# Decay rows of a pair loaded for both heads in one transfer: two transfers a pair instead of four

## The chip, the cores and the metric

One core of a Trainium2 chip runs the whole program. The time is the device time of one execution in microseconds; each version is run several times and the median counts. The engines are named as in the profile: PE is TensorE (matrix multiplications), with PEld for its weight loads; DVE is VectorE, ACT is ScalarE, POOL is GpSimd. SP is SyncE, which in this kernel does nothing but issue DMA transfers (its queue is SPq in the trace).

## The reference, cut to what matters

Three stages follow each other: causal attention with a decay, a feed-forward layer with a leaky ReLU, and a second layer with a softmax-gated activation and a layer norm. There are 4 batches of 8 heads, a sequence of 576 and a head dimension of 64; the 2304 tokens then go through matrices of 512 x 2048, 2048 x 512, 512 x 1024 and 1024 x 512. The change lies in the scores of the attention:

```python
scores = scale * np.matmul(q, k.transpose(0, 1, 3, 2))
log_f = np.log(np.clip(f, 0.0001, 1.0))
cum = np.cumsum(log_f, axis=-1)
decay = cum[:, :, :, None] - cum[:, :, None, :]
scores = np.where(causal, -1000000000.0, scores + decay)
scores = scores - np.max(scores, axis=-1, keepdims=True)
attn = np.exp(scores)
```

The decay of a score is a sum of a term of its query and a term of its key. So it can be had from the same matrix product that gives the scores, by a few more rows under the 64 rows of Q and K: these are the decay rows.

## The kernel before, in words

**Pairs and blocks.** The 32 heads are worked on in 16 pairs (two heads of one batch). A head's 576 queries are five blocks of 128 (the last has 64). Blocks 0 and 1 need only the first 256 keys. A pair is worked on twice: once for blocks 0 and 1 (pass kind "A", called full, since its scores are plain f32 matmuls), once for blocks 2, 3 and 4 (kind "B", called split: Q and K are split in two parts of lower precision first). `PASSES` (L41) lists eight passes of four pairs each, one for each batch and kind, with the priority of its first pair and the step from pair to pair: ("A", 0, 127.52, 0.5), ("A", 1, 186, 3), ("B", 0, 200, 5), ("A", 2, 222, 8), and so on. Pair 7 is the last pair of ("A", 1).

**Decay rows.** `decay()` (L504) computes the cumulative logarithms of all heads once and writes them to a tensor in DRAM, `dr_d` (L383), with four rows for each head: high and low parts of the decay, and ones, so laid out that the same four rows serve keys and queries in different columns. `row(h, p)` (L498) gives the index in `dr_d` of head h of pair p. The four writes are kept in `st["cols"]`, on which every load of decay rows depends.

**Loads of a full pair.** `prep_full` (L566) takes the four pairs of batch 0 from a tile of their own, `qa`, and returns. For the other 12 pairs it takes a `raw` tile (there are three, `NRAW`, L28), loads 64 rows of Q and K for both heads by one transfer from `kqa` (L575; 256 KB), and then rows 64 to 67 by four transfers from `dr_d` (L576 to L579): for each head one for the 256 keys (columns 0 to 255) and one for the 256 queries (columns 256 to 511), 4 KB each. The scores' matmuls (`qk_mm`, L639) then read 68 rows of one head's half of the tile. `raw` tiles are also what the split pairs (`prep_split`, L582) load their Q and K into (`raw<-kq`, 480 KB), and what stages weights later on. They are handed out in the order in which the code asks for them.

**What sets the order.** The code above issues nothing by itself. Each step is an operation in a `Plan` (L112) with an engine or a choice of engines, an expected duration, a priority and its dependences. `Plan.run` (L163) plays them through with its own model of time, and emits each instruction when the model gives it an engine: of those that are ready, the one with the lowest priority number, if its tiles can be had. That order of emission is each engine's order on the chip, where each engine and each DMA queue goes strictly in order. A transfer (`move`, L462; `load`, L466) takes 475 ns of SP in the model (L463), and at least 460 ns lie between two transfers (L289). A transfer is passed over while more than `BACKLOG` (L54) of expected DMA time is queued (L258), unless its priority is below -1000. A load's priority is that of its pair less `LD` = 51.31 (L48); that of a weight less `LDW` = 52.07 (L50); spills of results have the pair's less 400 and the transposes (`turn`, L469, used in `softmax`, L686) that less 500. All transfers go through SP (`QUEUES`, L99).

**Weights.** `load_wi` and `load_wo` (L821, L825) load weights of 512 KB through three `wst` tiles and turn them to two parts on ACT, DVE and POOL; chunk c has the priority 137.84 + 5.27 c (`wi`) or 148.79 + 5.27 c (`wo`), c up to 8 in the first half (L1037 to L1040). `ffn_a` (L891) computes the feed-forward layer's first half from them, between the attention's work.

Of the kernel before, what the change touches and what calls it, by code (L numbers as in the profile page):

```python
# [47 lines left out]
LD = 51.31  # L48
# [14 lines left out]
KB = CQ + 256  # L63
# [294 lines left out]
def body(tc, kqa, kq, vt, f, wa, w2i, w2o, gln, out):  # L358
# [24 lines left out]
    dr_d = dram.tile([2 * NP, 4, KQ], F32, name="dr_d")  # L383
# [78 lines left out]
    def move(dst, src, nbytes, prio, engs=QUEUES, **kw):  # L462
        d = {SP: 475.0, ACT: 490.0, POOL: 1040.0}  # L463
        return flex(engs, [d[e] for e in engs], lambda e: queue[e].dma_start(dst(), src()), prio, dma=nbytes / 360.0, **kw)

    def load(buf, dst, src, nbytes, prio, mode="w", **kw):  # L466
        return move(dst, src, nbytes, prio, **{mode: [buf]}, **kw)
# [30 lines left out]
    def row(h, p):  # L498

        return KD * h + p if p < KD else 2 * KD + (NP - KD) * h + p - KD  # L500
# [57 lines left out]
    st, QK, VT, U, QA = {}, {}, {}, {}, {}  # L558
# [7 lines left out]
    def prep_full(p, prio):  # L566


        if p < KD:
            bq = QA[0]  # L570
            QK[p] = [[(bq, p), (bq, "n"), (bq, "c")]] * 2, lambda hd: qa[0:66, hd, p], {0: 256, 1: 384}
            return
        bq = P.buf("raw")
        a = lambda r0, r1: bq.t[r0:r1, 0:1024].rearrange("r (h c) -> r h c", h=2)
        load((bq, 0), lambda: a(0, 64), lambda: kqa[p].rearrange("(h d) c -> d h c", h=2), 64 * 1024 * 4, prio - LD)  # L575
        for hd in range(2):  # L576
            for c0, k0 in ((0, 0), (256, KB)):
                load((bq, (hd, c0)), lambda hd=hd, c0=c0: a(64, 68)[:, hd, c0:c0 + 256], lambda hd=hd, k0=k0: dr_d[row(hd, p), :, k0:k0 + 256], 4096, prio - LD,
                     deps=st["cols"])  # L579
        QK[p] = [[bq]] * 2, lambda hd: a(0, 68)[:, hd], {0: 256, 1: 384}  # L580

    def prep_split(p, prio):  # L582
# [562 lines left out]
```

## Time and profile before

| | |
|---|---|
| Median of 3 runs | 848.83 us (846.91 to 849.77) |
| The profiled execution's own time | 848.65 us |
| Its span, first to last instruction | 846.9 us |
| PE busy | 767.9 us, 91% |
| DVE, ACT, POOL busy | 519.4, 490.1, 348.8 us |
| Mean granted clock of PE | 0.993 of full speed |
| DMA, mean | 128 GB/s, 52.3% of 16 engines' span |
| Decay loads `raw<-dr_d` | 48 of 4 KB |

The span is that of one profiled execution. Busy time is the time in which an engine has an instruction under way; an idle time is put down to the instruction or transfer whose end released the engine. Numbers in a row of the trace are microseconds unless they are marked ns. In the names, `raw<-dr_d` is a transfer into a `raw` tile from `dr_d`; `pt<-hl` is a transpose of softmax results.

### The profile page before, as it was taken

The numbers are of one execution on the slowest core, as the hardware profiler recorded it, in microseconds if no ns is written. First come the engines' busy times: TensorE is split into PE (matmuls) and PEld (weight loads), VectorE is DVE, ScalarE is ACT, GpSimd is POOL, SyncE is SP. The second block draws the span as 40 slices with busy tenths as digits, with TensorE's granted clock in tenths as the row PEclk, the third lists the DMA queues.
The fourth block names the chain that finished last, engine by engine and source line by source line (L and its number), as shares of the span: only waits on it lengthen the run. The fifth ranks groups of instructions, "written<-read, shape, count | busy, mean of one in ns | idle before, by whom it ended". The sixth has DMA issues, their size and how long they took to land.

```text
span 846.9 us, 16019 instructions
## 1 busy us (share of the span) xinstructions
PE 767.9 (91%) x5648; PEld 695.5 (82%) x5648; DVE 519.4 (61%) x1350; ACT 490.1 (58%) x1242; POOL 348.8 (41%) x448
## 2 busy tenths in 40 slices
PE   1753798979999999999899998999999999999996
PEld 1432698968998999999899987898889988998885
DVE  5788767888888878884654667334633434253551
ACT  4886768889889889884555543232333243333321
POOL 6648545166618564822610443422332233222321
PEclk9999999989999999999999999999999999999999
DMA  8997457687789677694655643321332131312223
GB/s 230 220 223 245 96 130 151 150 221 154 136 162 216 155 163 151 174 160 148 195 172 177 189 104 104 71 79 16 98 71 68 26 87 38 87 26 63 26 56 82
DMA packets 184402, 108.37 MB, mean 128 GB/s; under 512 B 150033, under 2 KB 167137, under 8 KB 184321
## 3 DMA queue, kind: packets, MB, share of 16 engines
q1 hardware_dynamic: 184320, 107.35, 52.3%
q8 instruction: 44, 0.72, 0.4%
q14 instruction: 38, 0.30, 0.1%
HBM read 57.39 MB, written 14.78 MB: 85 GB/s over the span
## 4 chain that ended last, share of the span: by engine, by line
PE 64%; DMA 10%; DVE 9%; ACT 8%; issue 4%; POOL 3%; SPq 0%; ACTq 0%; DVEq 0%; POOLq 0%
PE ps_f L473 40%; PE ph L473 10%; PE py L473 6%; PE ps_s L473 5%; PE ps_v L473 3%; ACT ps_s L657 2%; DMA raw<-w2o 2%; DMA tr<-hl 2%; DMA raw<-kq 2%; DMA wst<-wa 1%; DMA pt<-hl 1%; ACT hl L427 1%; DVE hl L438 1%; DMA qa<-sd 1%; DVE ps_s L707 1%
## 5 line engine op out<-in xcount | busy, mean ns | idle before, releaser
L473 PE MATMUL ps_f<-x,wi 128*128 128x256 f32 x972 | 131.7, 289 | 1.2 <-POOL x L442 1.1
L473 PE MATMUL ps_f<-g,wo 128*128 128x256 f32 x972 | 126.4, 284 | 2.5 <-DVE g L855 2.5
L473 PEld LDWEIGHTS ps_f<-x,wi 128*128 128x128 f32 x972 | 124.7, 193 | 3.1 <-POOL x L442 1.9
L473 PEld LDWEIGHTS ps_f<-g,wo 128*128 128x128 f32 x972 | 120.8, 188 | 4.0 <-DVE g L855 2.9
L473 PE MATMUL ph<-wi,g 128*128 128x512 f32 x408 | 98.5, 397 | 1.4 <-DVE raw L968 1.4
L473 PE MATMUL ps_f<-x,wib 128*128 128x256 f32 x756 | 97.3, 279 | 1.8 <-DVE g L855 1.7
L438 DVE SCALAR_TENSOR_TENSOR hl<-ps_s,st,hl 128x512 f16<-128x512 f32 (+4 forms) x160 | 82.8, 540 | 19.4 <-ACT hl L427 16.5
L473 PEld LDWEIGHTS ps_f<-x,wib 128*128 128x128 f32 x756 | 91.6, 188 | 2.9 <-DVE g L855 2.8
L473 PEld LDWEIGHTS ph<-wi,g 128*128 128x128 f32 x408 | 75.9, 188 | 19.3 <-DVE raw L968 1.6
L855 DVE TENSOR_TENSOR g<-ps_f,g 128x256 fp32r<-128x256 f32 x144 | 60.3, 420 | 48.1 <-ACT ps_f L854 47.2
L853 ACT ACTIVATE g<-ps_f 128x256 fp32r<-128x256 f32 x144 | 54.8, 380 | 59.3 <-PE ps_f L473 58.1
L657 ACT ACTIVATE ps_s<-ps_s,st 128x512 f32<-128x512 f32 (+4 forms) x160 | 78.6, 491 | 10.1 <-DVE st L707 6.1
L473 PE MATMUL ps_f<-wo,x 128*128 128x512 f32 x348 | 84.0, 396 | 0.0
L427 ACT ACTIVATE hl<-ps_s,st 128x512 f16<-128x512 f32 (+4 forms) x151 | 76.1, 532 | 11.6 <-DMA pt<-hl 4.7
L473 PE MATMUL ps_v<-pt,VT 128*128 128x128 f16 (+1 forms) x928 | 62.3, 220 | 20.0 <-DVE xr L742 9.0
L473 PE MATMUL py<-g,wob 128*128 128x256 f32 x567 | 75.6, 278 | 2.0 <-ACT g L427 2.0
L473 PEld LDWEIGHTS ps_f<-wo,x 128*128 128x128 f32 x348 | 64.8, 188 | 15.1
L473 PE MATMUL ps_s<-kq 128*128 128x512 f32 (+5 forms) x256 | 66.7, 380 | 11.6 <-DVE hl L438 5.5
L442 POOL TENSOR_TENSOR kq<-raw,kq 64x576 fp32r<-64x576 f32 (+1 forms) x53 | 67.9, 1283 | 21.5 <-ACT kq L427 15.2
L473 PEld LDWEIGHTS <-VT 128*128 128x128 f16 x928 | 50.0, 102 | 30.4 <-issue 15.4
L473 PEld LDWEIGHTS py<-g,wob 128*128 128x128 f32 x567 | 71.2, 188 | 4.3 <-ACT g L427 2.3
L707 DVE CUSTOM_DVE_ANT_0 ps_s<-ps_s,mask 128x256 f32<-128x256 f32 (+3 forms) x128 | 62.2, 496 | 5.9 <-PE ps_s L473 4.5
(159 smaller groups left out, 1221.7 us busy)
## 6 DMA issues: line engine op xcount, KB each, us to landing
wst<-wa SPq DMA_DIRECT2D x18, 512.0 KB
sd<-xs_d SPq DMA_DIRECT2D x32, 256.0 KB
raw<-kq SPq DMA_DIRECT2D x16, 480.0 KB
raw<-wa SPq DMA_DIRECT2D x14, 512.0 KB
raw<-yp_d SPq DMA_DIRECT2D x18, 256.0 KB
vr<-vt SPq DMA_DIRECT2D x13, 320.0 KB
raw<-w2i SPq DMA_DIRECT2D x8, 512.0 KB
raw<-w2o SPq DMA_DIRECT2D x8, 512.0 KB
```

The lines of the kernel that those rows point to most:

```text
L427: nc.scalar.activation(o, i, CP, scale=1.0 if scale is None else scale)
L438: nc.vector.scalar_tensor_tensor(o, a, scale, b, op0=ALU.mult, op1=ALU.subtract)
L442: (nc.vector if eng == DVE else nc.gpsimd).tensor_tensor(o, a, b, op=ALU.subtract)
L473: nc.tensor.matmul(o, lhsT=l, rhs=r, start=start, stop=stop)
L657: P.op(ACT, act(W, 1, True) + 93, lambda view=view, j=j, k=k: nc.scalar.activation(view(), view(), AF.Exp, bias=sts.t[:, j:j + 1], scale=- ...
L707: P.op(DVE, dve(W) + 130, lambda i=i, j=j, view=view: nc.vector.tensor_tensor_reduce(view(), view(), mask[:, 512 - 128 * i:640], -0.125, 3 ...
L853: P.op(ACT, act(n, 0, True), lambda: nc.scalar.activation(g.t[:, 0, 0:n], h(), AF.Prelu, scale=WSC, alpha=0.01), eprio, w=[(g, 0)], r=[ps])
L855: P.op(DVE, dve(n) + 60, lambda: nc.vector.tensor_tensor(g.t[:, 1, 0:n], h(), g.t[:, 0, 0:n].bitcast(F32), op=ALU.subtract), eprio, w=[(g, ...
```

## The change

The loop over the two heads goes. Keys and queries are each loaded for both heads by one transfer, from a slice of `dr_d` that takes the rows of head 0 and head 1 of the pair by a step, turned so that the four rows are outermost. The tile, its layout, the bytes, the priority and the dependences are the same; the two transfers are of 8 KB.

```diff
-        for hd in range(2):
-            for c0, k0 in ((0, 0), (256, KB)):
-                load((bq, (hd, c0)), lambda hd=hd, c0=c0: a(64, 68)[:, hd, c0:c0 + 256], lambda hd=hd, k0=k0: dr_d[row(hd, p), :, k0:k0 + 256], 4096, prio - LD,
-                     deps=st["cols"])
+        for c0, k0 in ((0, 0), (256, KB)):
+            load((bq, c0 + 1), lambda c0=c0: a(64, 68)[:, :, c0:c0 + 256], lambda k0=k0: dr_d[row(0, p):row(1, p) + 1:row(1, p) - row(0, p), :, k0:k0 + 256].rearrange("h r c -> r h c"),
+                 8192, prio - LD, deps=st["cols"])
```

## Rows read from the trace of the kernel before

**Rows 1.** Busy time by stage: stage, length, engines with instruction counts, granted clock, DMA.
```profile
58.00:65.00 7.00, 0.83 (x3) 0.57 (x4) 4.62 (x13) 5.76 (x16) 2.81 (x4) 1.00 0.97 308
65.00:92.00 27.00, 9.50 (x31) 5.77 (x30) 21.76 (x52) 17.72 (x38) 20.72 (x19) 1.00 0.63 205
...
172.00:204.00 32.00, 25.98 (x194) 22.63 (x191) 25.97 (x83) 27.50 (x77) 21.07 (x24) 0.84 0.84 197
...
275.00:400.00 125.00, 124.41 (x1183) 119.16 (x1183) 97.05 (x285) 102.92 (x276) 62.52 (x76) 1.00 0.70 156
...
500.00:820.00 320.00, 316.54 (x1968) 281.04 (x1967) 145.85 (x274) 108.37 (x234) 97.10 (x142) 1.00 0.27 62
```

In a row of this view the busy times are those of PE, PEld, DVE, ACT and POOL in this order; after them come the granted clock, the DMA engines' busy share and GB/s.

**Rows 2.** Waits of PE over the whole span: total, times, longest.
```profile
PE ps_s L473 <- DMA raw<-dr_d: 6.2, 1, 6.2
```

**Rows 3.** Timeline of PE, 57 to 93 us: start, length, instructions, idle before.
```profile
57.79 0.74 PE L473 MATMUL ps_s<-raw 68*128 68x128 f32 x2
64.69 2.48 PE L473 MATMUL ps_s<-raw 68*128 68x128 f32 x6 [6.17 <-DMA raw<-dr_d]
69.73 0.79 PE L473 MATMUL ps_s<-kq 128*128 128x512 f32 x1 [2.56 <-ACT kq L427]
...
92.41 2.91 PE L473 MATMUL ps_f<-x,wi 128*128 128x256 f32 x12
```

**Rows 4.** Timeline of SP's queue, 47 to 63 us: start and length of issues.
```profile
47.80 0.98 SPq L464 DMA_DIRECT2D wst<-wa  x2
48.87 0.67 SPq L464 DMA_DIRECT2D raw<-kqa  x1
49.59 0.48 SPq L464 DMA_DIRECT2D raw<-dr_d  x1
...
50.56 0.32 SPq L464 DMA_DIRECT2D raw<-dr_d  x1
...
57.74 0.33 SPq L464 DMA_DIRECT2D raw<-dr_d  x1
...
61.66 0.33 SPq L464 DMA_DIRECT2D raw<-dr_d  x1
62.04 0.34 SPq L464 DMA_DIRECT2D raw<-kq  x1
```

**Rows 5.** Waits of SP's queue from 18 to 66 us, the largest.
```profile
SPq L470 <- DVE hl L438: 5.2, 6, 1.6
```

**Rows 6.** The chain that ended last: start, length, what.
```profile
48.40 6.38 DMA wst<-wa
...
62.04 4.58 DMA raw<-kq
```

**Rows 7.** Issue durations on SP by transfer: ns min/median/max, first and last start.
```profile
L464 SPq DMA_DIRECT2D raw<-dr_d x48: 239/290/483, 20.8 to 250.6; - x48
...
L464 SPq DMA_DIRECT2D raw<-kqa x12: 607/640/672, 11.2 to 247.2; - x12
...
L464 SPq DMA_DIRECT2D sd<-xs_d x48: 359/419/1712, 63.2 to 725.8; - x48
...
L464 SPq DMA_DIRECT2D qa<-sd x2: 688/752/817, 7.3 to 10.2; - x2
```

**Rows 8.** Timelines of SP's queue and of PE, 97 to 260 us.
```profile
101.30 0.65 SPq L464 DMA_DIRECT2D raw<-dr_d  x2
...
161.15 0.39 PE L473 MATMUL ps_s<-raw 68*128 68x128 f32 x2
...
172.97 0.99 SPq L464 DMA_DIRECT2D raw<-kq  x1
...
250.08 0.81 SPq L464 DMA_DIRECT2D raw<-dr_d  x2
...
258.59 0.49 PE L473 MATMUL ps_s<-raw 68*128 68x128 f32 x2 [0.18 <-DVE hl L438]
```

## The prediction, made before the change was run

> **What bounds the kernel now.** I began with the share of busy time stage by stage [rows 1]. From 275 to 400 us TensorE is busy 124.41 of 125.00 us, and from 500 to 820 us 316.54 of 320.00: there the end is set by TensorE's own matmuls, and nothing that a load of 4 KB does can shorten them. What can be won lies where TensorE idles: 6.17 us of the stretch 58 to 65 us (it is busy 0.83 of 7.00), 17.50 us of 65 to 92 us, and 6.02 us of 172 to 204 us, where the granted clock's mean is also down to 0.84, so that part of the stretch ran on the lower of the two levels, after TensorE had begun to idle.
>
> Next, what TensorE waited for [rows 2]. Of all its waits, one is put down to a decay-row load: 6.2 us, once. So of the 48 loads of `raw<-dr_d`, at most the last one or two of one pair have ever held the matmuls up. TensorE's timeline [rows 3] gives the place. At 57.79 us it computes a first block of pair 7, the last of the four pairs of pass ("A", 1); then it idles 6.17 us until 64.69 and goes on with that pair's other three blocks. SyncE's timeline [rows 4] says why: pair 7's Q and K load goes out at 48.87, its four decay loads at 49.59, 50.56, 57.74 and 61.66. The first two are head 0's, the last two head 1's, which come 8 to 12 us later. The last lands some 3.0 us after its issue (61.66 to 64.69).
>
> Why so late? SyncE is not full: between 18 and 66 us it waits itself, most of all for the low halves of the softmax (`hl`) that its transposes move [rows 5]. The plan is what holds the loads back. It lets a transfer go only when its own account of queued DMA time is under BACKLOG (9115 ns, L258), and then the lowest priority number first. Pair 7's loads have 186 + 3 x 3 - 51.31 = 143.69. The weights come before them (`wi` up to 137.84 + 5.27 x 8 - 52.07 = 127.93, `wo` up to 138.88), and so do transposes and spills; the first split load `raw<-kq` of pass ("B", 0) has 148.69 and comes after them. Each decay load of pair 7 thus uses one of few openings, and the issue of `raw<-kq` follows directly behind the fourth one, at 62.04 [rows 4]. That load is on the chain that ended last [rows 6].
>
> **The change part by part.**
>
> Removed and added: 12 pairs x 4 issues of 0.290 us go, 12 x 2 issues of two heads come [rows 7]. No row shows the new form (4 partitions, two heads, 256 elements). Its bounds: 0.290 us, if a second head costs nothing, and 0.752 us, the dearest row of a form with more dimensions (`qa<-sd`). The row nearest in pattern is `raw<-kqa`, 0.640 us, since it too takes heads out of the outer dimension of DRAM; nearest in the piece of a partition is `sd<-xs_d`, 0.419 us, two pieces of 256 elements. I take the middle of these two, 0.53 us. With 0.05 us between issues a pair saves 4 x 0.34 - 2 x 0.58 = 0.20 us of SyncE (bounds: 0.68 saved, 0.24 lost; over 12 pairs +8.2 to -2.9 us). SyncE has waits of its own around most of these, which cover either sign; if that cover were gone, the -2.9 us would be the loss. On the chain stands one such issue alone, at 61.66 with its gap: 62.04 - 61.66 = **0.4 us** gained.
>
> Pair 7's wait: if the two new loads go where the first two went, the second is out by about 51 us. Ahead of it are the weights issued at 47.80; the chain has a weight transfer from 48.40 to 54.78 [rows 6]. Landing behind that and with the 3.0 us seen, it is there by 55 to 58 us, before TensorE's turn at 58.5 (64.69 - 6.17). So the 6.17 us wait goes. What is late next: `ACT kq`, for which TensorE waits until 69.73 [rows 3]. The idle time on TensorE is therefore not what is gained. Gained is that the softmax of three blocks moves to a stretch where its engines had room: from 58 to 65 us VectorE idles 7.00 - 4.62 = 2.38 us, ScalarE 1.24 us, while from 65 to 92 us VectorE is busy 21.76 of 27.00 us and passes everything that the first feed-forward matmul (92.41 us) needs. At best 2.4 us, at worst nothing; I take the smaller room, ScalarE's, **1.2 us**.
>
> The split load `raw<-kq`: two openings of the plan come free, so it may go at 57.74 instead of 62.04, 4.3 us earlier. But DMA is busy 0.97 of that stretch at 308 GB/s [rows 1]; 480 KB brought forward push the weights behind by 480/308 = 1.6 us. So 0 to 2.7 us; I take the middle, **1.4 us**.
>
> The other eight pairs of the passes ("A", 2) and ("A", 3): nothing waits for them. Pair 8's last decay load goes out at 101.30 us and its first matmul is at 161.15; even the last pair's (250.08) are 8.5 us before a matmul on `raw` at 258.59 [rows 8]. Gain or loss 0 beyond SyncE's time above; the cover is that the loads are early.
>
> Moved: everything, a little. The plan books 475 ns of SyncE and 460 ns of its DMA queue for each transfer (L463, L289), so 24 transfers are 11.4 us fewer in SyncE's planned time, and from the first of them (20.8 us [rows 7]) on all queues may be put in another order. The trace has no row for that; its bounds are those of the largest stall in the mixed stage, 172 to 204 us: 6.0 us given back or a second 6.0 us. I take 0.
>
> Sum: 0.4 + 1.2 + 1.4 = 3.0 us of the profiled execution's 848.65 (span 846.9, and 1.75 around it), 845.65. That execution lies 0.2 us under the median of 848.83, so against the runs 845.8. Bounds without a new order: 848.8 and 848.8 - 5.5 = 843.3.
>
> **The rivals.**
>
> (a) The whole wait comes off: after 92 us TensorE is dense, so if the feed-forward began 6.2 us earlier, the end would too: 842.6. For it: VectorE and ScalarE have idle time before 92 us. Against: the wait for `ACT kq`, and the 17.50 us idle up to 92 that no decay load causes.
> The Trainium skill, page "DMA: Bandwidth & Descriptors", section "Rules for kernel authors", says that many small transfers are to be joined, since under 64 KB one pays mostly overhead; its fit (section on the GpSimd path's DMA) has some 2.0 us fixed for each, which for 24 would be, as an estimate, 48 us. The trace disagrees with that as a price of time: 47 of 48 decay loads have no wait of TensorE to their name.
>
> (b) No change: VectorE, at 81% from 65 to 92 us, takes as long for its work whatever pair 7 does, and the weights pushed behind `raw<-kq` take back the rest; or the new issues cost 0.6 to 0.75 us and nothing is saved, so that the change halves a count and not a time: 848.8, 847 to 850.
>
> (c) Slower: another order of the queues makes a second gap like that of 172 to 204 us. There `raw<-kq`, issued at 172.97 [rows 8], came when TensorE had run out of what was ready; its slot of `raw` comes free only after the last matmul of a pair that held it. If the new order puts that last matmul, or a transpose, one turn later in front of such a load at another place, TensorE idles 6.0 us once more: 854.8; with the clock's share of that stretch (0.16 x 32.00 = 5.1 us at most) 859.9. It decides from the point where idle time of TensorE between 92 and 275 us grows by more than the 3.0 us won before 92. For it: the plan doesn't know the real landings; it put head 1's matmul of pair 7 where TensorE then stood 6.17 us. Against: a new order can as well ease that gap, and before 92 us the change only takes work from a queue.
>
> **How the numbers follow.** The forecast, 845.8, has 0.30; (a) 0.10; (b) 0.28; (c) 0.32. A measurement of this kernel can tell about 0.3%, 2.5 us, from no change; the forecast and (a) lie beyond it: faster 0.40, same 0.28, slower 0.32. The likeliest case's own range is 843.3 to 847.5. The whole range starts 2 us under (a), for an order that also eases the gap at 172 us, 840.5, and ends at 857, half way through (c)'s two prices: beyond these lie less than 2 in 10.
>
> **What would show it.** Right: 24 `raw<-dr_d` of 8 KB; no wait of TensorE on `raw<-dr_d` about 58 us; `raw<-kq` out before 62 us; the first feed-forward matmul some 3 us before 92.41; TensorE's busy time unchanged at 768. Issues of 0.5 to 0.6 us would bear out my price. Wrong: a first feed-forward matmul at 92 or later, or one earlier whose lead is gone by 275 us, with longer idle and a clock under 1.00 in the mixed stage; or a wait on `raw<-dr_d` still there, because the plan puts both loads late.

## The result, and the profile after

The changed kernel is slower: 856.51 us (median of 4 runs, 855.29 to 857.56) against 847.87 us for the kernel before (845.01 to 849.77). The ratio is 1.0104, with a 95% interval of 1.0068 to 1.0140. The profiled execution took 855.29 us, its span 853.5. One execution among all those below, the first of the kernel with four early transfers, took 1289.13 us at a mean granted clock of 0.626 and is left out of that kernel's figures.

What the change says it does, it does. First the issue durations of the changed kernel on SP's queue (ns min/median/max), to be read beside [rows 7]:

```profile
L464 SPq DMA_DIRECT2D raw<-dr_d x24: 242/318/547, 19.7 to 248.0; - x24
```

24 transfers in place of 48, and one with two heads takes 0.318 us where one with a single head took 0.290. Next SP's queue about 50 us, which answers to [rows 4] (start, length):

```profile
47.26 0.66 SPq L464 DMA_DIRECT2D raw<-kqa  x1
47.96 0.82 SPq L464 DMA_DIRECT2D raw<-dr_d  x2
...
51.64 0.38 SPq L464 DMA_DIRECT2D raw<-kq  x1
...
60.65 0.42 SPq L464 DMA_DIRECT2D raw<-kq  x1
```

All decay rows of pair 7 are out by 48.8 us, and the first split load goes out at 51.64 instead of 62.04. And PE's timeline, beside [rows 3]; it also has the longest gaps after 200 us:

```profile
64.90 1.22 PE L473 MATMUL ps_s<-kq 128*128 128x512 f32 x2 [2.65 <-POOL kq L442]
...
89.61 0.82 PE L473 MATMUL ps_v<-pt,VT 128*128 128x128 f16 x6 [6.42 <-POOL VT L442]
...
92.06 2.91 PE L473 MATMUL ps_f<-x,wi 128*128 128x256 f32 x12
...
267.50 0.49 PE L473 MATMUL ps_v<-pt,VT 128*128 128x128 f16 x6 [3.67 <-DVE xr L741]
...
408.99 11.42 PE L473 MATMUL ps_f<-x,wi 128*128 128x256 f32 x72 [3.87 <-DVE g L854]
...
518.43 8.36 PE L473 MATMUL ps_f<-wo,x 128*128 128x512 f32 x24 [3.44 <-ACT x L427]
```

The wait of 6.17 us on `raw<-dr_d` is gone. But the first feed-forward matmul stands at 92.06, where it was at 92.41, although attention began 1.3 us earlier in this execution. And there are gaps that the kernel before didn't have.

To see where the time went I cut each span at three events: the first attention matmul (`ps_s<-qa`), the first feed-forward matmul (`ps_f<-x,wi`), and the last spill of an attention result (`xs_d<-xr`). The time up to the first of them is set by the first loads and lies between 15.8 and 19.3 us in all profiled executions. Here is the stage view of the kernel before in these three parts (columns as in [rows 1]):

```profile
18.56:92.41 73.85, 38.96 (x141) 26.86 (x142) 57.06 (x185) 56.54 (x158) 47.44 (x50) 1.00 0.82 218
92.41:392.16 299.75, 287.86 (x2625) 270.65 (x2626) 240.14 (x759) 255.57 (x704) 150.06 (x183) 0.98 0.72 157
392.16:846.90 454.74, 440.58 (x2884) 397.67 (x2882) 211.94 (x384) 169.85 (x369) 139.38 (x194) 1.00 0.34 90
```

And of the changed kernel:

```profile
17.23:92.06 74.83, 41.10 (x155) 28.18 (x156) 60.27 (x201) 57.20 (x163) 53.59 (x58) 1.00 0.87 224
92.06:393.45 301.39, 287.48 (x2643) 273.10 (x2641) 242.89 (x752) 251.27 (x692) 142.34 (x179) 0.99 0.71 155
393.45:853.50 460.05, 442.63 (x2854) 398.26 (x2852) 204.88 (x377) 174.23 (x375) 138.98 (x194) 0.98 0.33 89
```

Up to the first feed-forward matmul it is 1.0 us longer, up to the last spill 1.6, after it 5.3. In the first part PE, DVE and POOL do more (155 matmuls for 141; DVE is busy 60.27 for 57.06 us, POOL 53.59 for 47.44): work came forward. The first matmul on `kq` did too: it starts 47.67 us after the first attention matmul (64.90 - 17.23), where it took 51.17 us before (69.73 - 18.56). But this lead of 3.5 us is gone by the first feed-forward matmul. In the last part fewer matmuls are left, 2854 for 2884, and they take longer.

Over the whole span PE is busy 771.7 us for 767.9 with the same matmuls, and idle 81.8 us (853.5 - 771.7) for 79.0. In the last part PE is busy 2.05 us longer with 30 matmuls fewer, and there its clock was lower: the stage view of the changed kernel about the gaps at 405 and 515 us has

```profile
409.00:425.00 16.00, 15.61 (x107) 15.40 (x108) 10.07 (x19) 8.05 (x21) 7.01 (x11) 0.82 0.55 184
515.00:518.40 3.40, 0.00 (x0) 0.00 (x0) 3.37 (x8) 2.44 (x7) 3.28 (x5) 0.82 0.56 140
518.40:530.00 11.60, 11.57 (x39) 9.26 (x40) 1.89 (x4) 3.05 (x5) 4.00 (x5) 0.76 0.36 90
```

a mean granted clock of 0.82 and 0.76: part of each stretch ran on 1.2 instead of 2.4 GHz, at and after the gaps of 3.87 and 3.44 us. The kernel before has a gap of 2.33 us at 414 us and none above 1.7 us about 505 to 516, and 1.00 there.

### The profile page after: what moved, and what is told of

The parts are those of the page before. It is cut to its first block, busy times and chain, and to the rows that moved or that the text cites. A ratio compares the mean times of both kernels' runs of the same rounds, so it can differ in the third digit from the quotient of the medians.

```text
span 853.5 us, 15985 instructions
## 1 busy us (share of the span) xinstructions
PE 771.7 (90%) x5648; PEld 699.9 (82%) x5648; DVE 517.8 (61%) x1347; ACT 490.8 (58%) x1242; POOL 346.0 (41%) x452
## 4 chain that ended last, share of the span: by engine, by line
PE 58%; DMA 12%; DVE 12%; ACT 8%; issue 6%; POOL 4%; SPq 1%; POOLq 0%; ACTq 0%; DVEq 0%
PE ps_f L473 35%; PE ph L473 9%; PE py L473 5%; PE ps_s L473 5%; DMA pt<-hl 3%; PE ps_v L473 3%; DMA tr<-hl 2%; DVE hl L438 2%; ACT hl L427 2%; DMA raw<-w2i 2%; DMA vr<-vt 2%; DVE ps_s L706 1%; DVE kq L430 1%; ACT ps_s L656 1%; DVE xr L741 1%
## 5 line engine op out<-in xcount | busy, mean ns | idle before, releaser
L473 PE MATMUL ps_f<-g,wo 128*128 128x256 f32 x972 | 128.3, 286 | 0.4 <-DVE g L854 0.4
L438 DVE SCALAR_TENSOR_TENSOR hl<-ps_s,st,hl 128x512 f16<-128x512 f32 (+4 forms) x160 | 81.8, 538 | 15.4 <-ACT hl L427 12.9
L473 PE MATMUL ps_f<-wo,x 128*128 128x512 f32 x348 | 86.7, 406 | 3.9 <-ACT x L427 3.9
L473 PEld LDWEIGHTS ps_f<-wo,x 128*128 128x128 f32 x348 | 66.6, 194 | 19.8 <-ACT x L427 4.2
L427 ACT ACTIVATE hl<-ps_s,st 128x384 f16<-128x384 f32 (+4 forms) x151 | 74.9, 533 | 13.5 <-DMA pt<-hl 6.6
L706 DVE CUSTOM_DVE_ANT_0 ps_s<-ps_s,mask 128x256 f32<-128x256 f32 (+3 forms) x128 | 62.5, 495 | 11.4 <-PE ps_s L473 10.0
L442 POOL TENSOR_TENSOR kq<-raw,kq 64x576 fp32r<-64x576 f32 (+1 forms) x51 | 64.2, 1261 | 9.2 <-ACT kq L427 5.9
```

The lines of the kernel that those rows point to most:

```text
L427: nc.scalar.activation(o, i, CP, scale=1.0 if scale is None else scale)
L438: nc.vector.scalar_tensor_tensor(o, a, scale, b, op0=ALU.mult, op1=ALU.subtract)
L442: (nc.vector if eng == DVE else nc.gpsimd).tensor_tensor(o, a, b, op=ALU.subtract)
L473: nc.tensor.matmul(o, lhsT=l, rhs=r, start=start, stop=stop)
L706: P.op(DVE, dve(W) + 130, lambda i=i, j=j, view=view: nc.vector.tensor_tensor_reduce(view(), view(), mask[:, 512 - 128 * i:640], -0.125, 3 ...
```

## The experiments

Theory A: the joined transfers are harmless or good, and the time is lost because the plan, which books 24 transfers fewer, puts all queues into another order. Rival B: the two-head transfers themselves cost it.

**Joined transfers in the old order.** The plan still sees four loads a pair; the first two emit the joined transfers, the other two nothing. All other instructions of every engine and queue stand in the order of the kernel before.

```diff
-                load((bq, (hd, c0)), lambda ...: a(64, 68)[:, hd, c0:c0 + 256], lambda ...: dr_d[row(hd, p), :, k0:k0 + 256], 4096, ...)
+                def emit(e, hd=hd, c0=c0, k0=k0):
+                    if hd == 0:
+                        nc.sync.dma_start(a(64, 68)[:, :, c0:c0 + 256], dr_d[row(0, p):row(1, p) + 1:..., :, k0:k0 + 256].rearrange("h r c -> r h c"))
+                flex(QUEUES, [475.0], emit, prio - LD, dma=4096 / 360.0, w=[(bq, (hd, c0))], deps=st["cols"])
```

> All instructions of every engine and queue in the order of the kernel before; only, each pair's decay rows go out in two transfers of 8 KB, at the places of head 0's two, and head 1's two places stay empty. Theory A (the new order of the plan costs the time, the joined transfers by themselves nothing): not slower than before, 842 to 849 us; TensorE's wait of 6.17 us at 58 us is gone; if the attention's end and not the start of the feed-forward holds the rest, 846 to 849, if the lead lasts, 842 to 845. Rival B (the two-head transfers themselves cost it, by their issue or landing): 853 to 858 us as in the changed kernel.

Measured: 845.66 us against 848.22 (ratio 0.9984, 0.9962 to 1.0005). Rival B falls. The stage view in the same three parts, and PE's timeline about 60 us:

```profile
16.55:87.59 71.04, 38.85 (x141) 26.78 (x142) 56.54 (x185) 56.46 (x158) 47.80 (x50) 1.00 0.82 227
87.59:386.68 299.09, 288.38 (x2625) 271.67 (x2626) 237.68 (x759) 255.63 (x704) 150.34 (x183) 0.97 0.70 157
386.68:841.20 454.52, 440.60 (x2884) 397.35 (x2882) 212.18 (x384) 169.15 (x369) 139.95 (x194) 1.00 0.34 90
```

```profile
53.86 2.50 PE L473 MATMUL ps_s<-raw 68*128 68x128 f32 x6 [0.83 <-DVE hl L438]
65.06 0.79 PE L473 MATMUL ps_s<-kq 128*128 128x512 f32 x1 [8.70 <-ACT kq L427]
```

The feed-forward starts 71.04 us after the attention, 2.8 us sooner than before; the rest is unchanged to 0.7 us. The second fence shows how little a wait on PE says of a gain: the 6.17 us on `raw<-dr_d` are gone, and PE waits 8.70 us for `ACT kq` in place of 2.56. What did come sooner is the split load, on SP's queue:

```profile
56.39 0.45 SPq L464 DMA_DIRECT2D raw<-kq  x1
```

Counted from the first attention matmul, it goes out 3.6 us sooner (39.84 us for 43.48), and the first matmul on `kq` starts 2.7 us sooner (48.51 for 51.17). So nearly all of the 2.8 us are there at that matmul.

**Four transfers in the new order.** Each joined transfer of the changed kernel is taken apart again where it stands:

```diff
-            load((bq, c0 + 1), ..., 8192, prio - LD, deps=st["cols"])
+            def emit(e, c0=c0, k0=k0):
+                for h in range(2):
+                    nc.sync.dma_start(a(64, 68)[:, h, c0:c0 + 256], dr_d[row(h, p), :, k0:k0 + 256])
+            flex(QUEUES, [475.0], emit, prio - LD, dma=8192 / 360.0, w=[(bq, c0 + 1)], deps=st["cols"])
```

> The order of the changed kernel, with each two-head transfer taken apart into two of 4 KB, issued one after the other at its place: four a pair again. Theory A: as slow as the changed kernel, 854 to 860 us, with gaps of TensorE and a lower clock about 265, 405 and 515 us. Rival B: back to 846 to 850 us.

Measured: 860.67 us, ratio 1.0160 (1.0134 to 1.0186). Slow as theory A has it, and above the changed kernel. All three gaps are there again, the last 3.75 us long at 520 us; the other two are, on PE's timeline:

```profile
270.55 0.80 PE L473 MATMUL ps_v<-pt,VT 128*128 128x128 f16 x6 [4.11 <-DVE xr L744]
...
414.91 10.40 PE L473 MATMUL ps_f<-x,wi 128*128 128x256 f32 x72 [3.93 <-DVE g L857]
```

So the order costs. That joined transfers help in this order too is likely, not certain: the two intervals just overlap (1.0140 and 1.0134).

**Four early transfers in the old order.** Here the first of the four loads emits the keys of both heads as two transfers, the second the queries; the other two emit nothing. The first expectation is for the timed runs, the second for one more profiled execution:

> The order of the kernel before and its four transfers of 4 KB a pair, but both heads' keys go out at the place of head 0's keys and both heads' queries at that of head 0's queries. Theory A and with it the thought that only the late rows of head 1 mattered, not the number of transfers: within 1.5 us of the joined transfers in the old order, 842 to 849 us, no wait of TensorE on decay rows at 58 us. If the number of issues matters: slower than that kernel by 24 issues of 0.3 us at most, 7 us.

> One look at the four early transfers in the old order. If only the late rows of head 1 mattered: no wait of TensorE on decay rows, the first feed-forward matmul 71 to 72 us after the first attention matmul, as with joined transfers, against 73.85 before. If the number of issues matters for it too: 73 to 74 us.

Measured: 847.78 us, ratio 1.0004 (0.9988 to 1.0020), which is 2.1 us above the joined transfers and not clear of them, since the intervals overlap. In the profiled execution PE has no wait on decay rows, and 72.98 us lie between the first attention matmul and the first feed-forward matmul. So by single executions the late rows were worth 73.85 - 72.98 = 0.9 us, and the number of issues 72.98 - 71.04 = 1.9 us. In the new order four instead of two cost 77.32 - 74.83 = 2.5 us in this stretch. The split is not firm: two more executions with joined transfers whose order is the old one this far have 72.58 and 72.15 us (below), which leaves 0.4 or 0.8 us for the number of issues in place of 1.9.

**Is it this new order or any?** The planned order was drawn anew without a change of the work, by the number of ns that the plan books for a transfer (L463): 470 and 480 for 475, in the kernel before and in the changed one.

```diff
-        d = {SP: 475.0, ACT: 490.0, POOL: 1040.0}
+        d = {SP: 470.0, ACT: 490.0, POOL: 1040.0}
```

> The kernel before with nothing changed but the number that the plan books for a transfer on SyncE, 470 instead of 475 ns: the same work and the same transfers in another order. Theory A1 (any new order costs about as much, the old one being a lucky draw): 852 to 860 us. Theory A2 (only the changed kernel's order is bad): 845 to 851 us.

> The kernel before, 480 instead of 475 ns booked for a transfer on SyncE: another order of the same work. If the old order is a lucky draw (A1): 852 to 860 us. If the draw with 470 was an unlucky one: 845 to 851.

> The changed kernel, 480 instead of 475 ns booked for a transfer on SyncE. If the changed kernel's order is one bad draw among others: anything from 846 to 860 us, other than 856.5 by 3 us or more. If joined transfers lead to slow orders by some rule: 854 to 860.

> The changed kernel, 470 instead of 475 ns booked for a transfer on SyncE: one more order from the start. If a new order of the first 95 us is dear as a rule and the order of the kernel before the rare good one: 852 to 864 us. If half of all orders are about as good as before: as likely 845 to 851.

Measured, as ratios to the kernel before: 1.0091 (1.0056 to 1.0127) and 1.0082 (1.0053 to 1.0112) for the four-transfer kernel with 470 and 480; 1.0189 (1.0158 to 1.0219) and 1.0186 (1.0141 to 1.0231) for the changed one with 480 and 470. 5 ns on a booked number, with the same matmuls and transfers, cost 0.8 to 0.9%, about as much as the change did. A new plan is more than a new order, though: it also gives some steps to another engine (with 470 in the kernel before DVE has 1356 instructions for 1350, ACT 1239 for 1242). The two were not separated, and "order" stands for both here.

**Which part of the order?** In two more kernels all transfers are joined, but the plan books two loads only for some pairs and four for the others, by `range(2 if p < 2 * KD else 1)` and the reverse; a third uses `3 * KD`.

> All transfers joined, but the plan knows of it only for pairs 8 to 15; for pairs 4 to 7 it still books four, of which two go out. The order is that of the kernel before until the loads of pair 8, about 95 us. Theory C (what costs lies in the order of the first 90 us): as the joined transfers in the old order, 843 to 849 us. Theory D (any new order of the mixed stage after 95 us costs as much): 852 to 860 us.

> All transfers joined, and the plan knows of it only for pairs 4 to 7: the order is that of the changed kernel for the first 115 issues of SyncE, then another one. Theory C: 853 to 860 us. Theory D, if this second order happens to be good: 845 to 851 us; if it is as bad as the two others tried, 853 to 860.

> All transfers joined, the plan knows of it only for pairs 12 to 15: the order of the kernel before up to their loads, about 195 us, then a new one. Theory C (only another order of the first 95 us is dear): 842 to 849 us. Theory D (any new order of the mixed stage costs, the one from 95 us on was luck): 851 to 860 us.

Measured: with the old order up to the loads of pair 8, 844.76 us, ratio 0.9958 (0.9937 to 0.9979): faster than both kernels. With the changed kernel's order for the start and another behind, 858.58 us, 1.0125 (1.0098 to 1.0152). After these two theory C looked right. The third refuted it: old order up to about 195 us, 859.39 us, 1.0128 (1.0096 to 1.0160). Its first part is good (72.15 us), and the loss comes later: 306.61 us up to the last spill and 461.53 us after it, with 2908 matmuls left. Not all of it can be put down to its new order. Up to about 201 us every engine still has the old order. PE's 1001st matmul, which starts there, comes 111.9 us after the first feed-forward matmul, and 109.1 us after it in the joined kernel of the old order. So 2.7 of the 7.5 us lost up to the last spill lie before the new order begins, and 4.8 us behind. So no one place of the order is to blame; theory D holds for it, and the kernel of 844.76 us is the one good draw.

**One hole taken by itself.** In the changed kernel the hole at 405 us shows DVE waiting for POOL's share in splitting the input of the last feed-forward block, in front of the hidden results for which PE waits. The splitting of that input got a later priority; PE's order stays the same to the last matmul, and DVE's changes only from about 400 us on.

```diff
-                copy_f(lambda x=x: x.t[:, 0], ..., TB, prio - 3000, w=[(x, 0)], r=[xw])
+                late = 1700 if blk == 8 and tag == "x" else 3000
+                copy_f(lambda x=x: x.t[:, 0], ..., TB, prio - late, w=[(x, 0)], r=[xw])
...
-                sub_f(..., TB, prio - 3000, ...)
+                sub_f(..., TB, prio - late, ...)
```

> The changed kernel; only the splitting of the last feed-forward block's input (block 8) has a later priority, -1700 for -3000, so that it no longer stands in VectorE's queue ahead of the hidden results of block 7. TensorE's order is the same to the last matmul, and all orders are the same up to about 400 us. Theory F (5 us of the loss is the two holes after the attention's end, the first of them VectorE held up by input that has not landed, and the lower clock behind it): 849 to 853.5 us, TensorE's wait of 3.87 us at 405 us down to under 2, the clock there at 1.00. Rival G (the holes only show time that would be lost anyway; the loss is of the first 95 us): 855 to 858 us.

Measured: 861.32 us, ratio 1.0155 (1.0126 to 1.0183). Neither came. The wait wasn't removed but cut in two, some 10 us apart, as PE's timeline has it:

```profile
410.32 6.22 PE L473 MATMUL ps_f<-x,wi 128*128 128x256 f32 x36 [2.05 <-DVE g L854]
419.96 5.24 PE L473 MATMUL ps_f<-x,wi 128*128 128x256 f32 x29 [3.42 <-DVE g L854]
```

This edit doesn't show what the hole is worth: the delay moved to the next results in the queue, 5.5 us of waiting for 4.3. And up to the last spill, where the order is still that of the changed kernel, this execution is already 2.5 us longer than the other.

**All of them in one table.** The ratio is of all runs. The three parts are of one profiled execution each, and PE's idle time is its span less its busy time. Executions of one kernel differ by some us (842.94 to 848.96 for the joined transfers in the old order, of which the fastest is the profiled one; the changed kernel's is its fastest too), so 2 or 3 us in a single cell prove little.

| kernel | ratio | start to feed-forward | to last spill | after it | PE idle | PE busy |
|---|---|---|---|---|---|---|
| before | 1 | 73.85 | 299.75 | 454.74 | 79.0 | 767.9 |
| joined, old order | 0.9984 | 71.04 | 299.09 | 454.52 | 72.9 | 768.3 |
| four early, old order | 1.0004 | 72.98 | 300.82 | 453.99 | 74.9 | 769.8 |
| plan for pairs 8 to 15 | 0.9958 | 72.58 | 298.57 | 454.48 | 77.6 | 767.3 |
| plan for pairs 12 to 15 | 1.0128 | 72.15 | 306.61 | 461.53 | 83.6 | 773.7 |
| changed | 1.0104 | 74.83 | 301.39 | 460.05 | 81.8 | 771.7 |
| four, new order | 1.0160 | 77.32 | 303.67 | 459.58 | 86.2 | 772.7 |
| plan for pairs 4 to 7 | 1.0125 | 75.72 | 303.18 | 459.97 | 85.1 | 771.6 |
| changed, late input | 1.0155 | 75.04 | 303.70 | 462.89 | 85.3 | 774.2 |
| before, 470 | 1.0091 | 79.08 | 308.91 | 453.13 | 90.3 | 768.5 |
| before, 480 | 1.0082 | 71.96 | 310.89 | 451.46 | 81.5 | 768.6 |
| changed, 480 | 1.0189 | 78.72 | 304.22 | 464.30 | 90.9 | 772.5 |
| changed, 470 | 1.0186 | 72.90 | 320.84 | 453.12 | 90.6 | 775.2 |

The first four rows spend 454 to 455 us after the last spill. The changed kernel spends 460, and so do, with 460 to 464, the four transfers in the new order, the plans for pairs 12 to 15 and 4 to 7, the late input and the changed one with 480. Both kernels of before with another number, and the changed one with 470, lose most of it between the feed-forward's start and the last spill instead (309 to 321 us).

## Why the prediction was wrong

**What held.** The late loads of head 1 were the cause of the 6.17 us, and that wait is gone, also where four loads go out early. The split load went out earlier, at 51.64 for 62.04. PE's idle time was not the gain: as foretold, `ACT kq` was late next in the old order. The sum for the transfers, 3.0 us, agrees within the noise with what they do by themselves: 1.3 to 2.8 us up to the first feed-forward matmul in three profiled executions (72.58, 72.15 and 71.04 us for 73.85), and a ratio of 0.9984, 1.4 us, at the end, whose interval reaches from 3.2 us gained to 0.4 lost. But that the sum came near is partly luck, for its terms are not what was gained. Of the 2.8 us in the joined kernel of the old order, 2.7 are there at the first matmul on `kq`. Read at that place, the split load's term of 1.4 us measured 2.7, its upper bound, and the 1.2 us for the softmax don't show. One price was off too: I took 0.53 us for the issue of a two-head load, nearest to forms with more partitions; measured are 0.318 us, near the lower bound of 0.290. A pair saves 4 x 0.34 - 2 x 0.37 = 0.62 us of SP and not 0.20.

**The step that failed** is the term under "Moved: everything, a little", which I took as 0 between bounds of 6.0 us to either side. The new order was not a small thing beside the three terms but the largest term. Against the joined transfers in the old order (824.65 us from the first attention matmul to the end) the changed kernel's order costs 3.8 us up to the feed-forward, 2.3 up to the last spill and 5.5 after it, 11.6 us in all in the profiled executions; by the ratios of all runs (1.0104 for 0.9984) it is some 10 us, and with four transfers (1.0160 for 1.0004) some 13. The eight new orders tried (the changed kernel's, the four with another booked number, the three with a part of the plan) gave seven ratios from 1.0082 to 1.0189 and one of 0.9958. They are not eight independent draws, since some begin alike: the plan for pairs 4 to 7 as the changed kernel, those for pairs 8 to 15 and 12 to 15 as the kernel before. Still, a zero in the middle of bounds was no neutral choice. That the old order is good beyond what a new one is likely to be was to be seen only by drawing others, which the trace of before can't show.

**The rivals.** The size was near that of rival (c), 854.8 us, to which I gave 0.32, and its mechanism was of the right kind (another order, longer gaps, lower clock); but its place was wrong, so that the size agrees by luck. From 172 to 204 us PE idles 3.43 us in the changed kernel (32.00 - 28.57), less than the 6.02 of before, and over 92 to 275 us its idle time is 11.4 us for 11.3. The loss is in the first part, where the split load went out at 51.64 us without the feed-forward starting sooner, and after 275 us: 125.00 - 121.67 = 3.33 us idle for 0.59 from 275 to 400, then the holes of 3.87 and 3.44 us with the low clock behind them. Rival (a), the whole wait as a gain, is refuted by the joined transfers in the old order. Rival (b), no change, is not excluded for those transfers alone, since their interval holds 1.
The Trainium skill (page "DMA: Bandwidth & Descriptors", section "Rules for kernel authors") says that many small transfers are to be joined, since under 64 KB one pays mostly overhead. The runs with the old order don't speak against it, but the gain isn't clear of noise: 24 transfers less gave 1.4 us, at most 3.2, which is 0.06 us each and at most 0.13. On the same page of the Trainium skill, the fit for transfers issued by GpSimd has some 2.0 us fixed for each; no such price shows in these runs.

**What stays open.** Why the old order is better than seven of eight others was not shown, nor where between the first `kq` matmul and the feed-forward the changed kernel lost its lead. An order of which many were tried and the best kept would look like this, but no run here tells that. Nor was the share of the hole at 405 us settled, since the edit that was to close it moved it.

## What to carry to other kernels

Where a planner or list scheduler writes the order of all queues, an edit that changes a booked cost or a count draws the whole order anew; cost it as a draw, with the spread that a few neutral changes of a booked number show (here, with 470 and 480, 0.8 and 0.9% slower than the kernel before, and 0.8% slower than the changed one), and not as zero. Test the edit itself with the order held: let the plan book what it booked before and only emit something else. Here that separated a gain of 1.4 us (3.2 gained to 0.4 lost) from a loss of some 10, and planning for the later pairs alone gave a kernel faster than the one before by 0.42% (0.21 to 0.63). That it is faster than the joined transfers in the old order is not shown, since those intervals overlap.

## What the runs showed of the hardware

A second head in a transfer of 4 partitions costs SP next to nothing: 0.318 us median in the changed kernel (0.304 in the old order) for 8 pieces of 1 KB, against 0.290 us for 4; the 64-partition load of two heads takes 0.64 us. And single gaps of PE of 3.4 us and more in the changed kernel, at 267, 405 and 515 us, each went with a stretch of lower clock about their end (a mean of 0.89 from 265 to 280 us, and 0.82 and 0.76 in the rows above); with the same number of matmuls, PE's busy time grew by 3.8 us, more than its idle time did (2.8 us).

One thing in the rows misleads: a clock of 1.00 before about 98 us, as in [rows 1] and in the first part of the stage views above, only says that no lower clock is on record there. In the kernel before the clock's record begins at 98.3 us, with 1.00. By the lengths of its matmuls PE ran on the lower level until then: six `ps_v<-pt,VT` matmuls took 0.82 us at 84.14 us, about as long as in a stretch recorded at the lower level (0.80 us at 187.31), and 0.51 us at 98.85. Twelve `ps_f<-x,wi` matmuls that took 2.91 us at 92.41 [rows 3] took on PE's timeline of the kernel before, later,

```profile
99.17 1.68 PE L473 MATMUL ps_f<-x,wi 128*128 128x256 f32 x12
```

By this reading the 14 matmuls that came forward into the first part of the changed kernel ran slower there than they would have later.
